# A fixed cycle for the pieces of each group of tokens, kept in strict order on each engine

## The chip, the cores and the metric

The program runs on one NeuronCore of one Trainium2 chip. The metric is the device time of one execution in microseconds (us), as the median of several runs. Engines are named as in the profile: PE (TensorE matmul), PEld (TensorE weight load), DVE (VectorE), ACT (ScalarE), POOL (GpSimd), SP (the queue that issues DMAs).

## The reference

Attention over pooled keys, then a feed-forward layer, both for every token:

```python
kv_pool = kv.reshape(B, H // r, r, W // r, r, C).mean(axis=(2, 4))   # r = 4
k = v = kv_pool.reshape(B, -1, C) @ w_sr                             # 768 keys per batch
s = scale * (q @ k.transpose(0, 2, 1))
a = softmax(s)
x = a @ v
h = x @ w_in                                                         # 128 -> 2048
out = (h - tanh(h)) @ w_out                                          # 2048 -> 128
```

There are 4 batches of 12288 tokens, C = 128. The kernel uses that scores and hidden values are small: it computes the softmax as a linear part (a 128x128 matrix applied to q) and what exp leaves beyond it, and h - tanh(h) around a centre as a slope, a square and a cube.

## The kernel before, in words

Tokens go in 96 groups of 512 (24 per batch). One group has these pieces; a "piece" of 1024 columns is two matmuls into one tile `big` of two PSUM banks, and there are three `big` tiles in a ring for all pieces of all groups.

Attention (function `attention`; the line numbers are those before the change):
- `load_q` (SP, L698) brings q, `rounded_q` (POOL, L701) makes the rounded copy `qr`.
- three times: `scores` (PE, L717) fills a `big`; `exps` (ACT, L721) reads it into E; `beyond` (DVE, L724) reads E and `big` into r2 and frees the `big`.
- `shares` (PE, L741, six narrow matmuls), `copy_shares` (ACT, L746), `all_shares` (PE, L749), `share_left` (ACT, L761, writes t): the denominators.
- `straight` with Mn (PE, L752, a plain fp32 product) and three times `values` (PE, L757) accumulate into one bank; `apart` (DVE, L768) multiplies it by t into dl; `rounded` (POOL, L771) makes dr.

The three accumulators (den4, den, num) share one PSUM bank, the ring `x` with one buffer, in which the small products of a batch's preparation take their turns too.

Feed-forward (function `feed_forward`), eight units:
- `forth` (PE, L810) fills a `big`; for units 1 to 7 `square` (ACT, L814) and `cube` (DVE, L817) make r and free the `big`; for unit 0 ACT copies it (L821) and POOL does the rest in three operations (L824, L828 twice).
- `back` (PE, L850) accumulates every unit into the bank `acc`, to which a plain product with A adds (`straight`, L798); `result` (ACT, L859) takes it to o, and SP stores it.

Keys (`keys`) and the weights around a centre (`about_centre`) of the next batch are prepared among the groups of the batch before: keys are pooled from 12 loads on DVE (L373) and POOL (L367), then small products on PE (L424, L433, L450, L503, L563, L665), DVE scales weights (L619).

The order is set at build time. Every piece of work is entered in `Plan` with a step number (one group is 8 steps), an engine, a duration, what it reads and writes. `Plan.run` plays the plan forward: each engine takes, among its pieces that could start within `SOON` of the earliest, the one with the lowest step. The order that comes out is the order of the instructions in each engine's queue; on the chip each engine goes through its queue, and semaphores hold an instruction until what it needs is done. Tiles of a ring are given out in the order of their steps.

Of the kernel before, what the change touches and what calls it, by code (L numbers as in the profile page):

```python
# [47 lines left out]
class Plan:  # L48

    HOP = 0.1  # L50
    OWN = {"DVE": 0.16, "ACT": 0.02}
    SOON = 0.15

    def __init__(self, tc):
        self.tc = tc
        self.ops, self.tiles, self.rings = [], {}, {}
        self.names = {}

# [11 lines left out]
    def op(self, step, engine, us, emit, reads=(), writes=(), late=0.0, port=False, dma=0.0,  # L70
           name=None):
        i = len(self.ops)
        self.ops.append((step, engine, us, emit, late, port or engine == "POOL", dma))
        self.names[name] = i
        for keys, writes_it in ((reads, False), (writes, True)):
            for k in keys:
                k, part = k if isinstance(k, tuple) else (k, None)
                self.tiles[k]["by"].append((i, writes_it, part))

    def run(self, between):  # L80
# [6 lines left out]
        for t in self.tiles.values():  # L87
            for j, (i, w, part) in enumerate(t["by"]):
# [62 lines left out]
def attention_then_ffn(ctx: ExitStack, tc: tile.TileContext, q, kv, w_sr, w_in, w_out, out):  # L151
# [23 lines left out]
    def sb(key, tag, shape, dt=F32, step=0.0):  # L175
# [509 lines left out]

    def attention(g, s0):
# [17 lines left out]
        plan.op(s0 - 10, "SP", 0.5, load_q, (), (qs,), late=2.0, dma=0.65)  # L704
        plan.op(s0 - 3, "POOL", 0.63, rounded_q, (qs,), (qr,))
        for k in range(AN):
            s, e, r = (f"{x}.{g}.{k}" for x in ("s", "e", "r2"))
            at = s0 + k * ATT / AN
            big(s, at)
            sb(e, "E", [P, WIDE])  # L710
            plan.tile(r, "r2", BUFS["r2"], lambda: wk.tile([P, 2 * WIDE], F16, tag="r2", name="r2",
                                                           bufs=BUFS["r2"])[:, 0:WIDE])
# [14 lines left out]
            plan.op(at - 6, "PE", 0.465, scores, (kTr, qr), (s,), late=0.2)  # L727
            plan.op(at, "ACT", 1.03, exps, (s,), (e,), late=0.1)
            plan.op(at, "DVE", 1.22, beyond, (s, e), (r,), late=0.08)
        at = s0 + ATT  # L730
# [20 lines left out]
        def straight():  # L751
            PE.matmul(out=plan[num], lhsT=plan[Mn], rhs=plan[qs], start=True, stop=False)  # L752

        def values(k):
            for h in range(2):
                n = 2 * k + h
                PE.matmul(out=plan[num], lhsT=plan[vvr][:, n], rhs=half(plan[f"r2.{g}.{k}"], h),  # L757
                          start=False, stop=(n == KT - 1))
# [11 lines left out]
        def rounded():  # L770
# [3 lines left out]
        plan.op(at, "PE", 0.5, shares, ["ident"] + [f"r2.{g}.{k}" for k in range(AN)], (den4,),  # L774
                late=0.2)
        plan.op(at, "ACT", 0.6, copy_shares, (den4,), (d4,), late=0.1)
        plan.op(at, "PE", 0.235, all_shares, ("ident", d4), (den,), late=0.2)
        plan.op(at, "ACT", 0.69, share_left, (den,), (t,), late=0.1)
        plan.op(at + 1, "SP", 0.5, store_left, (t,), (f"left.{g}",), late=2.0, dma=0.02)
        plan.op(at + 0.5, "PE", 0.93, straight, (Mn, qs), (num,))  # L780
        for k in range(AN):
            plan.op(at + 0.5, "PE", 0.465, partial(values, k), (vvr, f"r2.{g}.{k}"), (num,), late=0.2)
        plan.op(at + 0.5, "DVE", 0.69, apart, (num, t), (dl,), late=0.08)
        plan.op(at + 1, "POOL", 0.63, rounded, (dl,), (dr,))
# [4 lines left out]
    def feed_forward(g, s0):  # L789
# [5 lines left out]
        sb(o, "o", [P, G])  # L795

        def straight():
            PE.matmul(out=plan[acc], lhsT=plan[Am], rhs=plan[dl], start=(g > 0), stop=(g == 0))  # L798

        if g:  # L800
            plan.op(s0, "PE", 0.93, straight, (Am, dl), (acc,))
        for n in range(UN):
            hp, u, r, v, z = (f"{x}.{g}.{n}" for x in ("h", "u", "r", "v", "z"))
            s = s0 + n - (2 if n in ON_POOL else 0)
            big(hp, s)
# [24 lines left out]
            plan.op(s - 6, "PE", 0.465, forth, (winr, dr), (hp,), late=0.2)  # L830
            back_at = s + 2
            if n in ON_POOL:
                sb(r, "rp", [P, WIDE], R32)
                sb(v, "v", [P, WIDE])
                sb(z, "z", [P, WIDE])
                plan.op(s, "ACT", 1.03, copy, (hp,), (v,), late=0.1)
                plan.op(s, "POOL", 1.05, moved_pool, (v,), (z,))
                plan.op(s, "POOL", 2.4, partial(times, z, z, v), (z, v), (z,))
                plan.op(s, "POOL", 2.4, partial(times, r, z, v), (z, v), (r,))
                back_at = s + 5  # L840
            else:
                sb(u, "u", [P, WIDE])
                plan.op(s, "ACT", 1.03, square, (hp,), (u,), late=0.1)
                sb(r, "r", [P, WIDE], R32)
                plan.op(s, "DVE", 1.22, cube, (hp, u), (r,), late=0.08)

            def back(n=n, r=r):
                for h in range(2):
                    f = 2 * n + h
                    PE.matmul(out=plan[acc], lhsT=plan[Wr][:, f], rhs=half(plan[r], h),  # L850
                              start=(g == 0 and f == 0), stop=(g > 0 and f == FT - 1))

            plan.op(back_at, "PE", 0.465, back, (Wr, r), (acc,), late=0.2)

        if g == 0:
            plan.op(s0 + UN + 1, "PE", 0.93, straight, (Am, dl), (acc,), late=0.2)
# [7 lines left out]
        plan.op(s0 + UN + 2, "ACT", 0.69, result, (acc, G0), (o,))  # L864
# [280 lines left out]
```

## Time and profile before

| | |
|---|---|
| median of 3 runs | 1433.41 us (1432.98 to 1434.4) |
| the profiled execution's own time | 1434.69 us |
| its span, first to last instruction | 1433.0 us |
| granted TensorE clock, mean | 0.996 |
| busy: PE, DVE, ACT, POOL | 96%, 88%, 85%, 55% |

Busy time is the share of the span in which an engine has an instruction in work. Matmuls overlap, so PE's share is not a measure of how fast it goes; what a piece costs PE is seen from the distance between starts. Idle time in front of an instruction is given in brackets with the instruction that ended it.

### The profile page before, as it was taken

The page shows a single profiled execution, that of the slowest core. Times are in us where ns is not written, and L with a number is a line of the kernel's source. Part 1 is how long each engine was busy: PE and PEld are TensorE (multiplying, and loading weights), DVE is VectorE, ACT ScalarE, POOL GpSimd, SP SyncE. Part 2 cuts the span into 40 slices and gives each one's busy share as a digit, 9 for nine tenths or more (in the row PEclk, how much of TensorE's full clock was granted, in tenths as well). Part 3 has the DMA queues.
Part 4 walks back from the last instruction along what each step waited for, and adds up shares of the span by engine and source line. Part 5 has one row for each costly group of instructions (what it writes and reads, how often), then busy time and mean ns, then how long its engine had stood idle before and what let it go on. Part 6 is the DMA issues. An engine that isn't in the chain of part 4 may idle for free.

```text
span 1433.0 us, 17640 instructions
## 1 busy us (share of the span) xinstructions
PE 1376.5 (96%) x5920; PEld 852.7 (60%) x5920; DVE 1255.7 (88%) x1250; ACT 1212.2 (85%) x1395; POOL 787.1 (55%) x692
## 2 busy tenths in 40 slices
PE   5899999999999999999899999999999999999997
PEld 4565555666555556666555556666655556555554
DVE  7978888899988887899888888889888888888886
ACT  4768898887889898888789988888889898898996
POOL 4765453576745544667654545485545445555453
PEclk9999999999999999999999999999999999999999
DMA  9231111023311110123211111021111111111100
GB/s 353 86 107 38 45 38 38 30 67 119 132 38 37 38 44 31 52 82 122 92 37 45 38 37 38 30 60 45 38 45 37 37 39 37 45 37 37 37 23 31
DMA packets 40370, 84.54 MB, mean 59 GB/s; under 512 B 5232, under 2 KB 7408, under 8 KB 40272
## 3 DMA queue, kind: packets, MB, share of 16 engines
q1 hardware_dynamic: 40272, 83.34, 17.6%
q8 instruction: 49, 0.80, 0.2%
q14 instruction: 49, 0.40, 0.1%
HBM read 57.93 MB, written 25.39 MB: 58 GB/s over the span
## 4 chain that ended last, share of the span: by engine, by line
PE 75%; DVE 13%; POOL 4%; DMA 3%; issue 2%; ACT 2%; SPq 0%; DVEq 0%; POOLq 0%; ACTq 0%
PE big L810 23%; PE acc L850 18%; PE x L757 8%; PE big L717 7%; DVE r L724 6%; PE acc L798 5%; PE x L752 5%; PE x L741 3%; DVE dl L768 3%; DVE r L817 3%; DMA kc<-in_kv_dram 2%; PE x L749 1%; POOL kc L367 1%; POOL rp L828 1%; POOL z L828 1%
## 5 line engine op out<-in xcount | busy, mean ns | idle before, releaser
L817 DVE SCALAR_TENSOR_TENSOR r<-big,u 128x1024 fp32r<-128x1024 f32 x672 | 797.6, 1218 | 66.5 <-ACT u L814 57.7
L814 ACT ACTIVATE u<-big 128x1024 f32<-128x1024 f32 x672 | 682.9, 1036 | 107.1 <-PE big L810 100.6
L810 PE MATMUL big<-dr,winr 128*128 128x512 f32 x1536 | 579.8, 460 | 27.7 <-DVE r L724 17.6
L850 PE MATMUL acc<-r,Wr 128*128 128x512 f32 x1344 | 445.4, 424 | 1.1 <-DVE r L817 1.1
L810 PEld LDWEIGHTS big<-dr,winr 128*128 128x128 f32 x1536 | 262.3, 188 | 238.5 <-DVE r L817 74.1
L824 POOL TENSOR_SCALAR z<-v 128x1024 f32<-128x1024 f32 x96 | 100.4, 1046 | 544.2 <-ACT v L821 544.2
L724 DVE SCALAR_TENSOR_TENSOR r<-E,big 128x1024 f16<-128x1024 f32 x288 | 348.9, 1212 | 22.2 <-ACT E L721 20.1
L721 ACT ACTIVATE E<-big 128x1024 f32<-128x1024 f32 x288 | 296.1, 1028 | 38.2 <-PE big L717 33.4
L850 PEld LDWEIGHTS acc<-r,Wr 128*128 128x128 f32 x1344 | 251.4, 189 | 70.8 <-DVE r L817 2.8
L828 POOL TENSOR_TENSOR z<-z,v 128x1024 f32<-128x1024 f32 x96 | 230.5, 2401 | 7.6
L828 POOL TENSOR_TENSOR rp<-z,v 128x1024 fp32r<-128x1024 f32 x96 | 230.2, 2398 | 0.9
L717 PE MATMUL big<-qr,kTr 128*128 128x512 f32 x576 | 195.6, 422 | 2.5 <-DVE r L817 1.6
L757 PE MATMUL x<-r,vvr 128*128 128x512 f16 x576 | 174.0, 384 | 0.0
L717 PEld LDWEIGHTS big<-qr,kTr 128*128 128x128 f32 x576 | 100.9, 188 | 59.6 <-DVE r L817 34.4
L821 ACT COPY v<-big 128x1024 f32<-128x1024 f32 x96 | 97.4, 1015 | 30.7 <-PE big L810 30.7
L768 DVE TENSOR_TENSOR dl<-x,t 128x512 f32<-128x512 f32 x96 | 66.2, 690 | 52.0 <-PE x L757 51.4
L798 PE MATMUL acc<-dl,A 128*128 128x512 f32 x192 | 99.4, 599 | 0.6 <-ACT o L859 0.6
L752 PE MATMUL x<-q,Mn 128*128 128x512 f32 x192 | 99.2, 598 | 0.7 <-ACT t L761 0.7
L757 PEld LDWEIGHTS <-vvr 128*128 128x128 f16 x576 | 34.3, 98 | 81.4 <-issue 80.7
L850 PE MATMUL acc<-rp,Wr 128*128 128x512 f32 x192 | 75.5, 474 | 0.0
L859 ACT ACTIVATE o<-acc,G 128x512 f32<-128x512 f32 x96 | 65.4, 681 | 4.0 <-PE acc L850 3.6
L701 POOL TENSOR_SCALAR qr<-q 128x512 fp32r<-128x512 f32 x96 | 61.4, 640 | 5.2 <-PE x L757 3.2
(169 smaller groups left out, 835.8 us busy)
## 6 DMA issues: line engine op xcount, KB each, us to landing
q<-in_q_dram SPq DMA_DIRECT2D x96, 256.0 KB
out_dram<-o SPq DMA_DIRECT2D x96, 256.0 KB
kc<-in_kv_dram SPq DMA_DIRECT2D x38, 512.0 KB
r<-in_kv_dram SPq DMA_DIRECT2D x8, 512.0 KB
kc<-inverse SPq DMA_DIRECT2D x12, 256.0 KB
u<-in_moe_w_in_dram SPq DMA_DIRECT2D x3, 512.0 KB
u<-in_moe_w_out_dram SPq DMA_DIRECT2D x3, 512.0 KB
left<-t SPq DMA_DIRECT2D x96, 2.0 KB
```

The costliest lines, as they stand in the source:

```text
L717: PE.matmul(out=half(plan[s], h), lhsT=plan[kTr][:, n * P : (n + 1) * P], rhs=plan[qr], start=True, stop=True)
L721: A.activation(out=plan[e], in_=plan[s], func=AF.Exp)
L724: V.scalar_tensor_tensor(out=plan[r], in0=plan[e], scalar=-1.0, in1=plan[s], op0=ALU.add, op1=ALU.subtract)
L752: PE.matmul(out=plan[num], lhsT=plan[Mn], rhs=plan[qs], start=True, stop=False)
L757: PE.matmul(out=plan[num], lhsT=plan[vvr][:, n], rhs=half(plan[f"r2.{g}.{k}"], h), start=False, stop=(n == KT - 1))
L768: V.tensor_tensor(out=plan[dl], in0=plan[num], in1=plan[t], op=ALU.mult)
L798: PE.matmul(out=plan[acc], lhsT=plan[Am], rhs=plan[dl], start=(g > 0), stop=(g == 0))
L810: PE.matmul(out=half(plan[hp], h), lhsT=plan[winr][:, f * P : (f + 1) * P], rhs=plan[dr], start=True, stop=True)
L814: A.activation(out=plan[u], in_=plan[hp], func=AF.Square)
L817: V.scalar_tensor_tensor(out=plan[r], in0=plan[hp], scalar=1.0, in1=plan[u], op0=ALU.add, op1=ALU.mult)
L828: PL.tensor_tensor(out=plan[to], in0=plan[x], in1=plan[y], op=ALU.mult)
L850: PE.matmul(out=plan[acc], lhsT=plan[Wr][:, f], rhs=half(plan[r], h), start=(g == 0 and f == 0), stop=(g > 0 and f == FT - 1))
```

## The change

No instruction is added or removed; the numbers that set the order are others, and so is the rule.

1. `Plan.op` takes `lane=True`. All pieces of `attention` and `feed_forward` on PE, ACT, DVE and POOL are entered so (not the DMAs). In `run`, the lane pieces of one engine are sorted by step, and each may start only after the one ahead of it in that sort. Work of `keys`, `about_centre` and the rest is not in a lane and is placed by step as before.
2. A table `AT` gives each piece a step relative to its group's own, attention from 21 steps ahead of it (q's rounding 37.5) to the result 10.43 after. Every group has the same, also the first three, which before were further ahead.
3. Tiles in SBUF that lane pieces use (E, r2, o, u, r, rp, v, z) are given out by these steps too; before they came in order of entry.
4. The terms of both accumulations are entered in order of their steps, so the first and last of them carry start and stop: the plain products no longer come first.
5. Durations and delays in the plan are others (`HOP` 0 for 0.1, `SOON` 0.05 for 0.15, 1.137 for a cube instead of 1.22, and so on); they act only on the order.

```diff
-    HOP = 0.1
+    HOP = 0
-    SOON = 0.15
+    SOON = 0.05
...
+        if lane:
+            self.lanes.setdefault(engine, []).append((step, i))
...
+        for lane in self.lanes.values():
+            lane.sort()
+            for (_, i), (_, j) in zip(lane, lane[1:]):
+                behind[j].add(i)
...
+    AT = dict(
+        forth=[-1.25, 0.84, 1.42, 2.30, 3.73, 4.46, 5.34, 7.38],
...
+        shares=-13.40, copy_shares=-12.64, all_shares=-11.68, left=-11.16, straight=-10.37,
...
-        plan.op(s0 - 10, "SP", 0.5, load_q, (), (qs,), late=2.0, dma=0.65)
-        plan.op(s0 - 3, "POOL", 0.63, rounded_q, (qs,), (qr,))
+        plan.op(s0 + AT["rounded_q"] - 7, "SP", 0.5, load_q, (), (qs,), late=2.0, dma=0.65)
+        plan.op(s0 + AT["rounded_q"], "POOL", 0.59, rounded_q, (qs,), (qr,), lane=True)
...
-        bank(den4, "x", at - 0.1)
+        bank(den4, "x", s0 + AT["shares"])
-        bank(den, "x", at)
-        bank(num, "x", at + 0.5)
+        bank(den, "x", s0 + AT["all_shares"])
+        bank(num, "x", s0 + min(AT["straight"], *AT["values"]))
...
-            attention(g, g * UN - ahead(g))
+            attention(g, g * UN)
```

In the changed kernel's lines scores are L735, beyond L742, shares L758, all_shares L766, straight L769 and L819, values L774, apart L785, forth L829, cube L836, back L867, and L672 is the product that was L665.

First place: VectorE over one calm group late in the program, from one `apart` to the next. Before:

```order
L768 TENSOR_TENSOR dl<-x,t 128x512
L724 SCALAR_TENSOR_TENSOR r_11456<-E,big 128x1024
L817 SCALAR_TENSOR_TENSOR r<-big,u 128x1024
L724 SCALAR_TENSOR_TENSOR r_11473<-E,big 128x1024
L817 SCALAR_TENSOR_TENSOR r<-big,u 128x1024 x3
L724 SCALAR_TENSOR_TENSOR r_11527<-E,big 128x1024
L817 SCALAR_TENSOR_TENSOR r<-big,u 128x1024 x3
L768 TENSOR_TENSOR dl<-x,t 128x512
```

and with the change:

```order
L785 TENSOR_TENSOR dl<-x,t 128x512
L836 SCALAR_TENSOR_TENSOR r<-big,u 128x1024
L742 SCALAR_TENSOR_TENSOR r_11471<-E,big 128x1024
L836 SCALAR_TENSOR_TENSOR r<-big,u 128x1024 x3
L742 SCALAR_TENSOR_TENSOR r_11525<-E,big 128x1024
L836 SCALAR_TENSOR_TENSOR r<-big,u 128x1024 x3
L742 SCALAR_TENSOR_TENSOR r_11568<-E,big 128x1024
L785 TENSOR_TENSOR dl<-x,t 128x512
```

The seven cubes and three `beyond` are the same; a cube now follows `apart`, where a `beyond` did, and the three `beyond` stand further apart.

Second place: TensorE in the calm, from a group's third scores to the next group's shares. Before:

```order
L717 MATMUL big<-qr,kTr 128x512 x2
L850 MATMUL acc<-r,Wr 128x512 x4
L810 MATMUL big<-dr,winr 128x512 x2
L850 MATMUL acc<-r,Wr 128x512 x2
L810 MATMUL big<-dr,winr 128x512 x2
L850 MATMUL acc<-r,Wr 128x512 x2
L810 MATMUL big<-dr,winr 128x512 x2
L741 LDWEIGHTS share
L741 MATMUL x<-r_7307,share 32x512
```

and with the change:

```order
L735 MATMUL big<-qr,kTr 128x512 x2
L867 MATMUL acc<-r,Wr 128x512 x2
L829 MATMUL big<-dr,winr 128x512 x2
L867 MATMUL acc<-r,Wr 128x512 x2
L829 MATMUL big<-dr,winr 128x512 x2
L867 MATMUL acc<-rp,Wr 128x512 x2
L867 MATMUL acc<-r,Wr 128x512 x2
L829 MATMUL big<-dr,winr 128x512 x2
L758 LDWEIGHTS share
L758 MATMUL x<-r_7305,share 32x512
```

Before, four `back` and three `forth` stand between the scores and the shares, two of the `back` right after the scores; now it is four `back` and three `forth`, with two `back` together later, one of them that of unit 0 (from rp), which before came after the shares.

Third place: TensorE at a batch change, around a product of the next batch's slopes (x<-Wg,winT). Before:

```order
L850 MATMUL acc<-r,Wr 128x512 x2
L810 MATMUL big<-dr,winr 128x512 x2
L717 MATMUL big<-qr,kTr 128x512 x2
L665 MATMUL x<-Wg,winT 128x128 x4
L810 MATMUL big<-dr,winr 128x512 x2
L850 MATMUL acc<-r,Wr 128x512 x4
L810 MATMUL big<-dr,winr 128x512 x2
L563 MATMUL x<-hb,wout_69 128x1 x4
L810 MATMUL big<-dr,winr 128x512 x2
```

and with the change:

```order
L867 MATMUL acc<-r,Wr 128x512 x2
L766 LDWEIGHTS share
L766 MATMUL x<-d_3035,share 128x512
L829 MATMUL big<-dr,winr 128x512 x2
L867 MATMUL acc<-r,Wr 128x512 x2
L672 MATMUL x<-Wg,winT 128x128 x4
L867 MATMUL acc<-r,Wr 128x512 x2
L829 MATMUL big<-dr,winr 128x512 x2
L769 MATMUL x<-q,Mn 128x512
L735 MATMUL big<-qr,kTr 128x512 x2
```

Before, the product stood among scores and `forth`, outside the span in which the group's own denominators and values hold the ring `x`; now it stands between all_shares (L766) and the plain product (L769), both of which use that ring.

More of the change, by code (lines that the diff above doesn't have):

```diff
@@ L828, in times @@
                 PL.tensor_tensor(out=plan[to], in0=plan[x], in1=plan[y], op=ALU.mult)
-            plan.op(s - 6, "PE", 0.465, forth, (winr, dr), (hp,), late=0.2)
-            back_at = s + 2
+            plan.op(s0 + AT["forth"][n], "PE", 0.465, forth, (winr, dr), (hp,), late=0.196, lane=True)
+            first, then = s0 + AT["first"][n], s0 + AT["then"][n]
             if n in ON_POOL:
[L833 to L840, printed above, removed]
-            else:
[L842 to L845, printed above, removed]
@@ L847, in back @@
-            def back(n=n, r=r):
-                for h in range(2):
[L849 to L856, printed above, removed]
+                sb(r, "rp", [P, WIDE], R32, step=then)
@@ L1070, in attention_then_ffn @@
     VL = 1.0
-    def ahead(g):
-        if g < 3:
-            return LEAD + (38, 33, EXTRA2)[g]
-        return LEAD - max(0, g - (NGT - 12)) * RAMP
     for b in range(B):
```

95 lines of the change are left out of this document (61 added, 34 removed).

## The prediction, made before the changed kernel was run

> **What bounds the kernel now.** I read four views: the page (busy shares, the chain that ended last), the times of one line that runs once per group (L859, the result), the timeline of one calm group, and the table of waits over ten such groups.
>
> ```profile
> span 1433.0 us, 17640 instructions
> ...
> PE 1376.5 (96%) x5920; PEld 852.7 (60%) x5920; DVE 1255.7 (88%) x1250; ACT 1212.2 (85%) x1395; POOL 787.1 (55%) x692
> ...
> PE 75%; DVE 13%; POOL 4%; DMA 3%; issue 2%; ACT 2%; SPq 0%; DVEq 0%; POOLq 0%; ACTq 0%
> ```
>
> TensorE looks full, but its busy time counts matmuls from start to modelled end, and these overlap. So the question is what a group of 512 tokens costs, and what its matmuls need. The results give the first: each row has a count and the first and last start.
>
> ```profile
> L859 ACT ACTIVATE o<-acc,G x2: 687/689/691, 81.3 to 101.9; 128x512 f32<-128x512 f32 x2
> ...
> L859 ACT ACTIVATE o<-acc,G x10: 679/682/691, 101.9 to 224.6; 128x512 f32<-128x512 f32 x10
> ...
> L859 ACT ACTIVATE o<-acc,G x14: 678/680/692, 224.6 to 419.6; 128x512 f32<-128x512 f32 x14
> ...
> L859 ACT ACTIVATE o<-acc,G x14: 679/681/687, 542.6 to 739.4; 128x512 f32<-128x512 f32 x14
> ...
> L859 ACT ACTIVATE o<-acc,G x20: 677/680/682, 1134.6 to 1394.9; 128x512 f32<-128x512 f32 x20
> ...
> L859 ACT ACTIVATE o<-acc,G x4: 680/682/687, 1394.9 to 1426.8; 128x512 f32<-128x512 f32 x4
> ```
>
> A calm group takes 122.7/9 = 13.63 and 260.3/19 = 13.70 us, say 13.65. While the next batch is prepared, a group takes 195.0/13 = 15.0 and 196.8/13 = 15.1 us. The first interval is 20.6 us, the last three are 31.9 us together.
>
> What the matmuls need is read from starts that follow without a wait:
>
> ```profile
> 78.01 0.61 PE L741 MATMUL x<-r,share 128*32 128x512 f16 x6
> 78.55 1.66 PE L850 MATMUL acc<-r,Wr 128*128 128x512 f32 x6
> ...
> 80.27 1.02 PE L798 MATMUL acc<-dl,A 128*128 128x512 f32 x2
> 81.13 1.12 PE L752 MATMUL x<-q,Mn 128*128 128x512 f32 x2
> ...
> 1261.64 0.63 PE L850 MATMUL acc<-r,Wr 128*128 128x512 f32 x2
> ...
> 1262.11 0.62 PE L810 MATMUL big<-dr,winr 128*128 128x512 f32 x2
> ...
> 1262.56 0.59 PE L752 MATMUL x<-q,Mn 128*128 128x512 f32 x1
> ```
>
> Two pairs take 0.92 us, so a pair 0.46; the two plain fp32 products 0.86 each; the six narrow share matmuls 0.54; the single all_shares half a pair, 0.23. A group has 22 pairs (3 scores, 3 values, 8 forth, 8 back): 22 x 0.46 + 2 x 0.86 + 0.54 + 0.23 = 12.6 us; 12.7 with the pair at 0.465, which I use. So about 0.95 us of each calm group is TensorE waiting. (The Trainium skill, page "TensorE: Matmul & The Clock Gate", section "Back-to-back issue gap", gives N/2.4 + 2.5 ns for a warm matmul, 0.43 us for a pair; the sum would be 22 x 0.035 = 0.8 us lower, 11.9. The rows show 0.46 at a granted clock of 0.996, and the measurement decides.)
>
> The waits are at one place, over ten calm groups (1200 to 1336.4 us):
>
> ```profile
> PEld big L810 <- DVE r L817: 7.3, 29, 0.3
> PEld big L810 <- DVE r L724: 6.8, 19, 0.4
> ...
> PEld big L717 <- DVE r L817: 4.2, 10, 0.4
> ```
>
> 58 times in ten groups the weight load ahead of a refill of a `big` tile waits for the VectorE operation that reads the old contents. There are three such tiles and eleven pieces per group, so half the refills are late. That VectorE operation in turn is late because VectorE stood idle earlier. The rows of one such group give the price of every hop:
>
> ```profile
> 1249.39 3.49 DVE L817 SCALAR_TENSOR_TENSOR r<-big,u 128x1024 fp32r<-128x1024 f32 x3
> ...
> 1252.55 0.62 PE L717 MATMUL big<-qr,kTr 128*128 128x512 f32 x2
> ...
> 1253.01 0.60 PE L757 MATMUL x<-r,vvr 128*128 128x512 f16 x2
> ...
> 1253.20 1.03 ACT L721 ACTIVATE E<-big 128x1024 f32<-128x1024 f32 x1 [0.29 <-PE big L717]
> ...
> 1253.72 0.69 DVE L768 TENSOR_TENSOR dl<-x,t 128x512 f32<-128x512 f32 x1 [0.84 <-PE x L757]
> ...
> 1256.59 1.21 DVE L724 SCALAR_TENSOR_TENSOR r<-E,big 128x1024 f16<-128x1024 f32 x1
> ...
> 1257.86 0.73 PE L810 MATMUL big<-dr,winr 128*128 128x512 f32 x2
> ...
> 1259.65 1.03 ACT L814 ACTIVATE u<-big 128x1024 f32<-128x1024 f32 x1
> ...
> 1260.71 1.22 DVE L817 SCALAR_TENSOR_TENSOR r<-big,u 128x1024 fp32r<-128x1024 f32 x1 [0.64 <-ACT u L814]
> ...
> 67.20 1.95 ACT L814 ACTIVATE u<-big 128x1024 f32<-128x1024 f32 x2 [0.33 <-PE big L810]
> ```
>
> TensorE start to ScalarE start: 0.65. ScalarE start to VectorE start: 1.06. VectorE start to the refill's start: 1.27. VectorE spacing back to back: (3.49 - 1.22)/2 = 1.13; ScalarE spacing: 1.95 - 1.03 = 0.92. A refill that waited lasts 0.73 instead of 0.62, since its weights were not loaded ahead: 0.11 us of TensorE each. VectorE is idle 0.84 before `apart` and 0.64 before a cube here; its own work is 10 x 1.13 + 0.69 = 12.0 us, ScalarE's at most 1212.2/96 = 12.6. TensorE is thus the largest sum, but the ring of three tiles sets the period.
>
> **The change, part by part.** No instruction is added or removed. Everything is order, so each term is a time between results.
>
> Calm groups. In the new cycle the tightest refill is that of the next group's first scores, which takes the bank of unit 1. The path: third scores, exps, beyond, cube of unit 1, refill: 0.65 + 1.06 + 1.13 + 1.27 = 4.11 us. In the same stretch TensorE has 8 pairs and the shares: 8 x 0.46 + 0.54 = 4.22. The refill of unit 7's bank is the other: from the third scores through six full and three half ScalarE operations (6 x 0.92 + 3 x 0.5, the half ones an estimate from the full one), then 0.65 + 1.06 + 1.13 + 1.27, 11.1 us in all, against 19 pairs, two plain products, shares and all_shares, 11.2. So both come due about 0.1 us ahead, where the old order has six late refills per group. `apart` comes right after the last values, 0.7 us from their start as now (1253.01 to 1253.72); VectorE has 0.7 us to spare per group (12.7 - 12.0). I take TensorE's 12.7 plus one weight load uncovered, 0.1: 12.8 us. Bounds: 12.7 (nothing late) and 13.65 (nothing gained); it is nearest the lower, because the two chains fit by the rows. What hides VectorE's 12.0 us and ScalarE's is now TensorE's work itself; if one of them slips, there is nothing behind it to fill the gap, since each lane is strict. Late next would be `apart`, and behind it the cube of unit 7.
>
> Batch changes. Three times the next batch's keys and weights are prepared among the groups. Their prices:
>
> ```profile
> 30.49 3.73 PE L503 MATMUL acc<-col,win 128*128 128x1 f32 x32 [0.25 <-DVE col L420]
> 34.08 1.80 PE L424 MATMUL big<-kvp,wsr 128*128 128x384 f32 x4
> 35.68 2.76 PE L433 MATMUL big<-wsr,kvp 128*128 128x128 f32 x12
> 38.09 1.43 PE L717 MATMUL big<-qr,kTr 128*128 128x512 f32 x4
> ...
> 603.45 0.95 PE L563 MATMUL x<-hb,wout 128*128 128x1 f32 x8
> 604.26 0.71 PE L810 MATMUL big<-dr,winr 128*128 128x512 f32 x2
> ...
> L619 DVE TENSOR_TENSOR winr<-win,kc 128x512 fp32r<-128x512 f32 x4 | 4.9, 1234 | 0.0
> ...
> L373 DVE TENSOR_REDUCE kvp<-kc 128x64 f32<-128x1024 f32 x6 | 7.3, 1210 | 1.6 <-DMA kc<-in_kv_dram 1.6
> ```
>
> TensorE: L503 3.6, L424 1.6, L433 2.4, and 76 small ones (L563, L665, L450) at 0.81/8 = 0.1: 15.3 us per batch. VectorE: 7.3 + 4.9 and about 2 of small ones, 14. With TensorE full, its 15.3 all lie on the path. VectorE has 0.7 us to spare per group, 9 over the 13 groups, so about 5 of its 14 come on top. Of the fifteen small products that borrow the one-bank ring `x`, about seven now fall between a group's shares, all_shares and values, where the old order had hardly any room between; each must be drained by VectorE, at up to 1.13 us of waiting, before the next matmul in line, partly under the pair that stands between (0.46): some 0.6 us each, 4 to 5 us. Sum 25 us per batch over the calm period. Bounds: 15.3 (all else hidden) and 15.3 + 14 + 7 x 1.13 = 37. I stay in the middle, since VectorE's slack is real but the insertions are lumps.
>
> POOL, SP: the q loads and roundings are issued some 14 steps earlier, but a tile of q is reused only when the plain product of four groups before has read it; POOL is 55% busy and its result is now wanted 6 steps (some 10 us) after `rounded`. Cost nothing; if a load comes late, the two multiplies behind it on POOL move, and `back` of unit 0 has 8 us of room.
>
> Start. Second result 101.9 us now, with 7 us in the first interval beyond a calm group. Attention of groups 0 and 1 is no longer pulled ahead of the weights, and no forth may pass the second scores of group 2. I take 98; bounds 95 (all 7 gone) and 104 (two more VectorE operations ahead of the first result).
>
> End. The last three intervals stay 31.9, which is 6.5 less than three of 12.8; the closing test costs 0.9 (260.3 against 19 x 13.65), and 6.2 us follow the last result (1433.0 - 1426.8).
>
> Sum: 98 + 94 x 12.8 (1203.2) + 3 x 25 (75) + 0.9 - 6.5 + 6.2 = 1376.8 us of span. This execution took 1434.69 us beside its span of 1433.0, and the median of the runs is 1433.41, 0.4 above the span: 1377 us.
>
> **Rivals.** All late refills vanish, and VectorE's extra work finds room: period 12.7, 16 per batch, start 95: 95 + 1193.8 + 48 + 0.6 = 1337. For it: both chains fit. Against: both fit by 0.1 us only.
>
> Batch changes at the upper bound, 37 each: 1377 + 36 = 1413. For it: two L672 products stand directly ahead of the plain product that needs their bank. Against: the old order paid only 15.0 - 13.65 = 1.4 us per group there, little over TensorE's share.
>
> The period is set by the hops, not the order, and stays 13.65 with the old losses: about 1433, no change. Against: VectorE's idle 0.84 and 0.64 in the row come from values and squares ordered late.
>
> Slower: in a strict cycle without slack every refill comes a little late, so each of the eleven pays its weight load: 12.7 + 11 x 0.11 = 13.9, which gives 98 + 1306.6 + 75 + 0.6 = 1480. It decides from a period of 13.4, that is seven of eleven late. For it: six are late today; 0.1 us of room in two chains is as large as the weight load. Against: nine others have more room, and lateness of VectorE shrinks as soon as TensorE slows. Half of it, five late, gives 13.25 and 1419. (The same page of the Trainium skill, section "Architectural detail", says that TensorE only pulls weight loads ahead and keeps matmuls in order, and that the other engines are strict queues; the 0.73 against 0.62 agrees. By that rule a late piece delays all behind it, which speaks for this rival.)
>
> **The numbers.** Forecast (1352 to 1402) 0.52; floor 0.16; dear batch changes 0.11; five late 0.09; unchanged 0.04; slower 0.08. A difference under 0.2% (2.9 us) can't be told from none. The range 1340 to 1418 leaves out the slower, the unchanged, the five late and the lowest tail. Faster 0.88, same 0.04, slower 0.08.
>
> **What would show it.** L859 at a spacing near 12.8 in calm stretches, near 14.7 in batch changes; waits of the weight loads for VectorE far under 18 us in ten groups; L819 and L829 with few idle notes; VectorE idle under 1 us per group. Wrong if calm spacing stays over 13.3, or if after each L672 the plain product waits 2 us or more.

## The result and the profile after

| | before | changed |
|---|---|---|
| median | 1433.91 us (4 runs, 1432.98 to 1434.84) | 1393.53 us (4 runs, 1391.8 to 1394.07) |
| ratio | | 0.9716, 95% interval 0.97 to 0.9733 |
| profiled execution: time, span | 1434.69, 1433.0 | 1394.07, 1392.3 |
| mean granted TensorE clock | 0.996 | 0.983 |

The change takes 40 us off, 2.8%. The forecast was 1377, 16.5 lower, with 1340 to 1418 around it. The same rows of the page as before, now of the changed kernel:

```profile
span 1392.3 us, 17512 instructions
...
PE 1345.4 (97%) x5920; PEld 871.9 (63%) x5920; DVE 1276.1 (92%) x1250; ACT 1203.2 (86%) x1395; POOL 784.6 (56%) x692
...
PEclk8779999999999999999999999999999999999999
...
PE 85%; DVE 6%; DMA 3%; ACT 2%; POOL 2%; issue 1%; SPq 0%; ACTq 0%; POOLq 0%; DVEq 0%
```

TensorE's share hardly moves, VectorE's rises from 88% to 92%, and in the chain VectorE falls from 13% to 6%. What has no counterpart before is the clock row: in the first three slices of 35 us the granted clock is well below full, where before it read 9 throughout:

```profile
PEclk9999999999999999999999999999999999999999
```

The result's starts (L878, one per group; count, then first and last start) give the time by stage:

```profile
L878 ACT ACTIVATE o<-acc,G x2: 680/682/685, 106.9 to 123.3; 128x512 f32<-128x512 f32 x2
...
L878 ACT ACTIVATE o<-acc,G x9: 674/685/688, 123.3 to 226.2; 128x512 f32<-128x512 f32 x9
...
L878 ACT ACTIVATE o<-acc,G x16: 681/688/689, 226.2 to 440.6; 128x512 f32<-128x512 f32 x16
...
L878 ACT ACTIVATE o<-acc,G x7: 682/682/688, 440.6 to 517.6; 128x512 f32<-128x512 f32 x7
...
L878 ACT ACTIVATE o<-acc,G x12: 687/688/688, 1200.5 to 1341.5; 128x512 f32<-128x512 f32 x12
```

The second result, at 101.9 before, now comes at 123.3: 21.4 us are lost at the start. A calm group takes 77.0/6 = 12.83 and 141.0/11 = 12.82 us. The fifteen groups of the first batch change take 214.4, that is 21.7 over fifteen calm ones taken at 12.845 (the median interval); the other two changes cost 21.1 and 18.2 in the same way. Measured between the same results before, the three changes became 8.0, 12.9 and 9.2 us shorter and the calm stretches and the end 32.0 together; less the 21.4 at the start that is the 40.7 between the spans.

The waits of the weight loads for VectorE in 14 calm groups (1109 to 1288 us):

```profile
PEld big L829 <- DVE r L836: 5.9, 27, 0.2
PEld big L735 <- DVE r L836: 5.5, 13, 0.4
```

40 late refills in 14 groups, 11.4 us; before it was 58 in ten groups, 18.3 us. Per group 2.9 instead of 5.8, and 0.8 us instead of 1.8.

Where the start goes shows in the timeline of TensorE (start, length, engine and line, count, and in brackets the idle time and what ended it):

```profile
49.88 0.39 PE L758 MATMUL x<-r,share 128*32 128x512 f16 x2 [1.73 <-DVE r L742]
...
53.27 0.61 PE L758 MATMUL x<-r,share 128*32 128x512 f16 x2 [1.87 <-DVE r L742]
...
56.63 2.07 PE L769 MATMUL x<-q,Mn 128*128 128x512 f32 x2 [1.15 <-ACT t L778]
...
71.28 1.25 PE L829 MATMUL big<-dr,winr 128*128 128x512 f32 x2
...
78.71 1.16 PE L672 MATMUL x<-Wg,winT 128*128 128x128 f32 x8 [0.57 <-DVE A L678]
81.16 1.05 PE L570 MATMUL x<-hb,wout 128*128 128x1 f32 x8 [1.30 <-DVE A L678]
82.47 2.07 PE L672 MATMUL x<-Wg,winT 128*128 128x128 f32 x8 [0.25 <-DVE G L577]
84.93 1.87 PE L570 MATMUL x<-hb,wout 128*128 128x1 f32 x8 [0.38 <-DVE A L678]
87.04 1.87 PE L570 MATMUL x<-hb,wout 128*128 128x1 f32 x8 [0.25 <-DVE G L575]
89.16 1.87 PE L570 MATMUL x<-hb,wout 128*128 128x1 f32 x8 [0.25 <-DVE G L575]
91.28 1.04 PE L758 MATMUL x<-r,share 128*32 128x512 f16 x6 [0.25 <-DVE G L575]
```

Two things. Up to 71 us the attention of the first groups goes through the engines one step at a time, with TensorE waiting for each; the first `forth` starts at 71.28 (before at 55.97). Then six of the first batch's eight small products stand in a row (78.71 to 91.28), each waiting until the one ahead has left the single bank of ring `x`. The next group's shares use that ring too and come behind them, and in the strict order nothing of the cycle may pass the shares. ScalarE shows it as one hole:

```profile
92.36 0.59 ACT L763 CAST d<-x 128x512 f16<-128x512 f32 x1 [14.31 <-PE x L758]
```

Before the change the first `forth` came early, and the same eight products stood apart, with `forth`, scores and `back` between them:

```profile
55.97 0.70 PE L810 MATMUL big<-dr,winr 128*128 128x512 f32 x2 [1.09 <-DVE r L724]
...
71.01 0.71 PE L810 MATMUL big<-dr,winr 128*128 128x512 f32 x2
71.55 1.15 PE L665 MATMUL x<-Wg,winT 128*128 128x128 f32 x8
72.46 0.71 PE L717 MATMUL big<-qr,kTr 128*128 128x512 f32 x2
73.01 0.62 PE L810 MATMUL big<-dr,winr 128*128 128x512 f32 x2
73.47 0.95 PE L563 MATMUL x<-hb,wout 128*128 128x1 f32 x8
```

The eight matmuls that take 0.95 here (L563) take 1.87 in the last three of that row (L570); the granted clock there is treated in the last section.

### The profile page after: what moved, and what is told of

Its sections match the earlier page's. It is cut to its first block, busy times and chain, and to the rows that moved or that the text cites. A ratio compares the mean times of both kernels' runs of the same rounds, so it can differ in the third digit from the quotient of the medians.

```text
span 1392.3 us, 17512 instructions
## 1 busy us (share of the span) xinstructions
PE 1345.4 (97%) x5920; PEld 871.9 (63%) x5920; DVE 1276.1 (92%) x1250; ACT 1203.2 (86%) x1395; POOL 784.6 (56%) x692
## 4 chain that ended last, share of the span: by engine, by line
PE 85%; DVE 6%; DMA 3%; ACT 2%; POOL 2%; issue 1%; SPq 0%; ACTq 0%; POOLq 0%; DVEq 0%
PE big L829 24%; PE acc L867 23%; PE big L735 10%; PE x L774 9%; PE x L769 6%; PE acc L819 6%; PE x L758 3%; DVE r L836 2%; DVE r L742 2%; PE x L766 2%; DMA kc<-in_kv_dram 1%; ACT E L739 1%; PE x L570 1%; ACT u L833 1%; DVE kvp L380 1%
## 5 line engine op out<-in xcount | busy, mean ns | idle before, releaser
L836 DVE SCALAR_TENSOR_TENSOR r<-big,u 128x1024 fp32r<-128x1024 f32 x672 | 798.2, 1218 | 32.6 <-ACT u L833 26.9
L829 PE MATMUL big<-dr,winr 128*128 128x512 f32 x1536 | 568.5, 451 | 4.6 <-DVE r L742 2.7
L867 PE MATMUL acc<-r,Wr 128*128 128x512 f32 x1344 | 423.8, 408 | 1.1 <-DVE r L836 1.1
L843 POOL TENSOR_SCALAR z<-v 128x1024 f32<-128x1024 f32 x96 | 101.0, 1052 | 513.8 <-ACT v L840 513.8
L742 DVE SCALAR_TENSOR_TENSOR r<-E,big 128x1024 f16<-128x1024 f32 x288 | 351.1, 1219 | 39.6 <-ACT E L739 17.9
L829 PEld LDWEIGHTS big<-dr,winr 128*128 128x128 f32 x1536 | 276.8, 190 | 129.9 <-DVE r L836 38.0
L867 PEld LDWEIGHTS acc<-r,Wr 128*128 128x128 f32 x1344 | 251.7, 188 | 65.3 <-DVE r L836 2.4
L735 PE MATMUL big<-qr,kTr 128*128 128x512 f32 x576 | 232.1, 484 | 1.0 <-ACT winr L658 0.7
L774 PE MATMUL x<-r,vvr 128*128 128x512 f16 x576 | 175.9, 388 | 0.0
L735 PEld LDWEIGHTS big<-qr,kTr 128*128 128x128 f32 x576 | 101.9, 190 | 97.7 <-issue 44.0
L769 PE MATMUL x<-q,Mn 128*128 128x512 f32 x192 | 100.4, 604 | 2.4 <-ACT t L778 2.3
L819 PE MATMUL acc<-dl,A 128*128 128x512 f32 x192 | 99.5, 600 | 0.6 <-ACT o L878 0.6
L774 PEld LDWEIGHTS <-vvr 128*128 128x128 f16 x576 | 33.9, 99 | 79.4 <-issue 79.2
L785 DVE TENSOR_TENSOR dl<-x,t 128x512 f32<-128x512 f32 x96 | 66.3, 691 | 9.8 <-PE x L774 4.9
L763 ACT CAST d<-x 128x512 f16<-128x512 f32 x96 | 56.4, 587 | 19.0 <-PE x L758 19.0
L878 ACT ACTIVATE o<-acc,G 128x512 f32<-128x512 f32 x96 | 65.9, 686 | 5.9 <-PE acc L867 5.7
L758 PE MATMUL x<-r,share 128*32 128x512 f16 x576 | 59.8, 389 | 7.4 <-DVE r L742 6.0
```

What stands on the lines that cost most here:

```text
L735: PE.matmul(out=half(plan[s], h), lhsT=plan[kTr][:, n * P : (n + 1) * P], rhs=plan[qr], start=True, stop=True)
L742: V.scalar_tensor_tensor(out=plan[r], in0=plan[e], scalar=-1.0, in1=plan[s], op0=ALU.add, op1=ALU.subtract)
L758: PE.matmul(out=plan[den4][at : at + QUAD], lhsT=share[:, 0:QUAD], rhs=half(plan[f"r2.{g}.{k}"], h), start=(n < 4), stop=(n + 4 >= KT), ti ...
L829: PE.matmul(out=half(plan[hp], h), lhsT=plan[winr][:, f * P : (f + 1) * P], rhs=plan[dr], start=True, stop=True)
L836: V.scalar_tensor_tensor(out=plan[r], in0=plan[hp], scalar=1.0, in1=plan[u], op0=ALU.add, op1=ALU.mult)
L867: PE.matmul(out=plan[acc], lhsT=plan[Wr][:, 2 * n + h], rhs=half(plan[r], h), start=(start and h == 0), stop=(stop and h == 1))
```

## The experiments

Twelve kernels, each a variation of the changed one. Each ratio is to the kernel before, run on the same chip beside it (1433.9, 1433.3 and 1434.3 us in the three sets of runs); the changed kernel has 0.9716.

### The start

**Attention of groups 0 and 1 entered earlier** (e1_early):

```diff
-            attention(g, g * UN)
+            attention(g, g * UN - (36, 31, 0)[g] if g < 3 else g * UN)
```

> The changed kernel, with attention of groups 0 and 1 entered 36 and 31 steps earlier (as far ahead as the order before the change had them); all else, the strict lanes too, as in the change. Theory A (the start lost its 21 us in two parts: attention of the first groups begins after the weights' products and then runs piece after piece in a strict lane with TensorE idle and its clock down, and eight small products stand in one row in the bank ring x): the first part goes, so the first result comes near 97 us instead of 106.9 and the time is near 1384. Rival B (the first groups are limited by the sum of work ahead of the first result, however ordered): the first result stays within 2 us of 106.9, time 1393. Rival C (what is gained at the start is given back because the later groups then wait): first result near 97, time 1393.

1389.71 us, 0.9692 (0.9676 to 0.9708); first result at 101.8, second at 118.5. Of the 9.5 us that theory A expected, 3.8 came, so none of the three theories fits. In this run's timeline attention begins earlier, but the first `forth` still starts at 71.38, and the next group's shares still come behind the row of products, at 86.95.

**The eight small products spread** (e2_spread): two of the slopes' products go ahead of the first group's units and two among them, the four of L570 behind them.

```diff
-        slopes_at = [known + 7 + AS * n if b else n / 2 - SL for n in range(4)]
-        value_at = [known + 5 + AS * n if b else n / 2 + VL for n in range(4)]
+        slopes_at = [known + 7 + AS * n if b else (-6.5, -6.3, 0.6, 0.8)[n] for n in range(4)]
+        value_at = [known + 5 + AS * n if b else 8.6 + n / 8 for n in range(4)]
```

> The changed kernel, with the first batch's eight small products in the ring x (L672 four times, L570 four times) given other steps: two of L672 between the values of group 0 and the shares of group 1, two after group 1's values, the four L570 after group 2's values; all else as in the change. Theory A: the stretch from 78.7 to 91.3 us of the profile, in which TensorE does little but these products one by one, shrinks from 12.6 to about 4 us, and the first result comes near 97 us, time near 1385. Rival D (these products are slow only because TensorE's clock is halved there, and the halved clock comes from the thin work before): the products keep about 2 us each wherever they stand, time 1390 or more.

1382.28 us, 0.9639 (0.9623 to 0.9655). The result's row, and one of the products with a `forth` right behind it:

```profile
L878 ACT ACTIVATE o<-acc,G x2: 681/684/687, 94.3 to 112.3; 128x512 f32<-128x512 f32 x2
...
87.44 0.95 PE L570 MATMUL x<-hb,wout 128*128 128x1 f32 x8
88.25 0.70 PE L829 MATMUL big<-dr,winr 128*128 128x512 f32 x2
```

11 of the 21 us lost at the start come back, and nothing else moves (batch changes 22.2, 21.3, 18.6). So parting the row of products gives back half of the loss. The product lasts 0.95 again, so rival D, by which each keeps about 2 us wherever it stands, falls; the clock in the start rose along with it, though (last section).

**Both edits** (e3_both):

> Both edits of the start together: attention of groups 0 and 1 earlier, and the eight small products spread. Theory A: the two losses add, the first result comes near 86 us, time near 1374 (1393.5 - 20), granted clock near 1 from 50 us on. Rival (the two are one loss seen twice): the time is that of the better of the two alone.

1384.84 us, 0.9657 (0.9641 to 0.9673), second result at 114.9: 2.6 us longer than the spread alone. The two causes don't add; with the products apart, earlier attention gains nothing.

**Groups 0 to 2 out of the strict order** (e9_lane3), in all entries of `attention` and `feed_forward`:

```diff
-            plan.op(s0 + AT["scores"][k], "PE", 0.465, scores, (kTr, qr), (s,), late=0.196, lane=True)
+            plan.op(s0 + AT["scores"][k], "PE", 0.465, scores, (kTr, qr), (s,), late=0.196, lane=g >= 3)
```

> Groups 0 to 2 are freed from the strict cycle (each engine may take their pieces by step number as other work allows); from group 3 on nothing changes. Theory S (part of the 25 us at the start is the strict order itself: scores, shares and values of groups 0 and 1 go in turn through the three engines while TensorE waits up to 1.9 us per hop): the two groups overlap, the first result comes 5 to 12 us before 106.9, the second 5 to 10 us before 123.3, total 1382 to 1389. Rival W (the attention waits for the weights' products, and the eight small products in a row hold the rest, whatever the order of the cycle): first and second result within 2 us of the changed kernel's, total 1392 to 1396. Calm period 12.82 and the batch changes 21, 21, 18 in both.

1385.17 us, 0.9669 (0.9652 to 0.9685); first result at 97.3, second at 115.0, with the steps of the products left as they are. So strictness itself costs 8 us here, as theory S expected. Without it other pieces come between the products, ahead of the waiting shares:

```profile
81.77 1.71 PE L570 MATMUL x<-hb,wout 128*128 128x1 f32 x8
83.33 1.20 PE L867 MATMUL acc<-r,Wr 128*128 128x512 f32 x2
84.33 1.70 PE L570 MATMUL x<-hb,wout 128*128 128x1 f32 x8
```

**Spread, and groups 0 to 2 free** (e12_lane2):

> The eight small products spread, and groups 0 to 2 freed from the strict cycle. Theory A (two causes in the start, the hold by the products and the strict order): first result 86 to 90, total 1374 to 1379. Rival B (one stretch of TensorE's wait, which either edit fills): first result 92 to 96, total 1380 to 1386.

1381.96 us, 0.9644 (0.963 to 0.9657). The first result in its profiled execution is earlier still (90.9), the second 109.5, but over five runs the time is that of the spread alone. By the total, rival B holds: there is one stretch of waiting, and either edit fills much the same part of it. The first result lies between the ranges of the two theories.

### Strictness against the table of steps

**No strict order anywhere, the new steps kept** (e4_nolane):

```diff
         if lane:
-            self.lanes.setdefault(engine, []).append((step, i))
+            pass
```

> The whole strict cycle is taken away, the new step numbers stay. Theory C (the calm gain of 0.83 us a group comes from the fixed order): order by step numbers lets refills of big drift late again, the calm period goes back to 13.2 to 13.7, total 1425 to 1475, though the start is 5 to 10 us shorter. Rival N (the new step numbers alone give the calm gain, the strictness only fixes what they would give anyway): calm within 0.1 of 12.82, the start shorter by 5 to 10 us, total 1382 to 1390.

1390.59 us, 0.9688 (0.966 to 0.9716), four runs between 1384.15 and 1394.72. Neither theory was right as a whole: the start is 7 us shorter (second result 116.3), and the calm period doesn't go back to 13.2 but to 12.98 in two of its stretches, and stays at 12.82 in the rest:

```profile
L878 ACT ACTIVATE o<-acc,G x7: 680/681/682, 433.4 to 511.3; 128x512 f32<-128x512 f32 x7
```

77.9 for six groups against 77.0. So of the 0.83 us that a calm group gained about 0.7 come from the new step numbers (and the plan's new durations, which no run took apart from them) in those two stretches, and all of it in the others; strictness adds 0.16 in the two, 2.8 us over their 19 groups. In the profiled execution the program without strict order is 7.0 us shorter at the start and 7.8 longer after it: those 2.8, and the rest in the batch changes and at the end. That execution is the longest of the four; their median is 2.9 us below the changed kernel's, so over the whole program no gain of strictness is shown.

### What sets 12.8 us

**The plain product with Mn left out** (e5_nostraight): 0.86 us of TensorE's work less in every group; the linear part of the attention is missing from the output.

```diff
-        terms.append((AT["straight"], 0.857, straight, (Mn, qs)))
```

> The plain fp32 product with Mn is left out (so the linear part of the attention is missing from the output); nothing else changes. It costs TensorE 0.86 us a group and no other engine anything. Theory T (TensorE's own work sets the calm period, everything else just fits): the calm period falls by most of 0.86, to 12.0 to 12.3, until VectorE's 12.0 us of work per group takes over. Rival H (the hops through the three big tiles set it): 12.6 to 12.85, since the hops don't get shorter.

1380.31 us in one run. Twelve calm results (L877 there):

```profile
L877 ACT ACTIVATE o<-acc,G x12: 687/688/689, 1188.6 to 1329.3; 128x512 f32<-128x512 f32 x12
```

140.7/11 = 12.79 instead of 12.82. Theory T falls: 7% less work on TensorE shortens the calm group by 0.03. (Of the 13 us in the total about half are the start, where the second result comes at 116.4.) The chain of waits of this run over one group shows what holds it:

```profile
1246.57 0.70 PE big L828 x2
...
1251.57 0.95 PE acc L866 x4
...
1253.13 1.02 ACT u L832
...
1256.92 1.04 ACT u L832
...
1257.99 1.24 DVE r L835
...
1259.36 0.70 PE big L828 x2
```

A loop: a refill of `big` and 6 us of TensorE in its order up to the last `back`; the result and then squares and exps on ScalarE without a gap, to 1257.96; one cube; and the next group's refill, 12.79 us after the last. The product with Mn doesn't lie in this loop. In the changed kernel the chain from 1160 to 1183 us is TensorE from end to end:

```profile
1160.91 0.54 PE x L758 x6
1161.45 0.67 PE big L735 x2
...
1166.86 0.45 PE big L735 x2
```

Its pairs take 0.46 there, which makes the 12.6 of TensorE's own work; the one dearer pair is the next group's first scores, a late refill at 0.67, and with these 0.2 it is 12.8. From 1210 to 1338 us (busy times of PE, PEld, DVE, ACT, POOL, then the granted clock), first of the changed kernel, then without Mn:

```profile
1210.00:1338.00 128.00, 128.00 (x551) 81.68 (x550) 123.54 (x111) 121.10 (x141) 68.77 (x50) 1.00 0.11 38
...
1210.00:1338.00 128.00, 126.13 (x531) 76.16 (x530) 122.87 (x111) 121.85 (x142) 68.79 (x48) 1.00 0.09 30
```

TensorE has no idle time in the first, and 1.87 us in the second. So two limits stand 0.03 us apart: TensorE's work with that late refill, and this loop through three engines. That the loop holds 12.79 is shown; that TensorE would stay at 12.8 with a shorter loop is not, since no run shortened it.

### The batch changes

**Small products out of the gap between shares and values** (e6_ring): the preparation's steps are shifted so that none falls between a group's shares, all_shares and values.

```diff
-    FS, AS, WS, APART, MORE = 3, 8, 6, 3, 3.0
+    FS, AS, WS, APART, MORE = 4, 8, 6, 3, 3.0
-    KEYS, ABOUT, GAP = 105, 85, 8
-    KEYS1, ABOUT1, GAP1 = 80, 60, 6.5
+    KEYS, ABOUT, GAP = 106, 86, 8
+    KEYS1, ABOUT1, GAP1 = 82, 62, 6.5
```

> The changed kernel with the steps of the three later batch preparations moved by 1 or 2, and the four first products 4 steps apart instead of 3, so that each small product in the ring x falls after a group's values and ahead of the next group's shares, and none between shares, all_shares and values. Theory E (of the 21 us that a batch change costs, 15 to 16 are TensorE's own work and the other 5 are matmuls held in line behind a small product's bank): a batch change costs about 17, time near 1381. Rival F (the rest is VectorE's extra work, which stays): time within 2 us of 1393.5. Rival G (what a product costs is that it takes TensorE while the other engines run dry, wherever it stands): no change either, but VectorE waits right behind each product.

1406.26 us, 0.9798 (0.9782 to 0.9815): 13 us longer than the changed kernel, which none of the three theories expected; the changes cost 25.4, 27.2 and 22.3. The trace has no small product left in that gap, where the changed kernel has eight of the fifteen in each change. In the groups that lose most, VectorE's scaling of weights meets POOL's products:

```profile
957.66 4.46 DVE L626 TENSOR_TENSOR winr<-win,kc 128x512 fp32r<-128x512 f32 x2
...
959.40 1.86 POOL L668 TENSOR_TENSOR Wg<-wout,hb 128x512 f32<-128x512 f32 x1
```

**The same, with scaling and POOL's products at their old steps** (e7_ring2): on top of the last edit:

```diff
+        late = b and min(b, 2)
-        winr_at = known + 8 if b else s0
+        winr_at = known + 8 - late if b else s0
```

and `late` is taken from the steps of `third_at`, `first_order` and `by_first` likewise.

> As the run that moved the small products out of the gap between shares and values, but the steps of the scaling of winr, the slopes' third operand and the first-order part stay where the changed kernel has them, so that VectorE's scaling (two SBUF inputs) no longer meets POOL's products of two SBUF inputs. Theory K (that run's 12.7 us of loss is the meeting of these operations, 4.46 us for two scalings against some 2.0): batch changes 19 to 22, total 1388 to 1395. Theory R (the ring of x tiles: small products out of the gap save 3 us per change once the meeting is gone): 1382 to 1388. Rival Q (the moved steps themselves cost, by what else they displace): 1400 to 1407 again.

1401.97 us, 0.9785 (0.9768 to 0.9801); changes 24.8, 24.4, 19.9. That is in rival Q's range, but the steps alone did not part the two kinds of work, so theories K and R were not put to the test. The scaling starts 17 us after its load was issued, and what put it there no run shows:

```profile
308.17 1.07 SPq L620 DMA_DIRECT2D kc<-inverse  x2
...
325.38 4.47 DVE L627 TENSOR_TENSOR winr<-win,kc 128x512 fp32r<-128x512 f32 x2
```

So what the gap in ring `x` costs stays open in these runs: neither separates it from the meeting. What they do show is that a shift of the preparation by one or two steps costs 1.7 to 6.1 us a change.

**All pooling of batches 1 to 3 on POOL** (e8_pool):

```diff
-            if (j % 2 if b else j % 3 == 2):
+            if (b or j % 3 == 2):
```

> The pooling of the key and value blocks of batches 1 to 3, of which every second step goes to VectorE (L380, 3 to 4 us of VectorE in a batch change), goes to POOL altogether. Theory V (half of a batch change is VectorE work that displaces the fixed order by its own length: groups 18 and 19 lose 2.5 and 1.0 us where four L380 stand): the second and third batch change drop from 21 and 18 to 15 to 18 each, total 1386 to 1390. Rival P (batch changes are TensorE's own extra products, 15 us, and ring waits; VectorE's extra work fits into its 8% idle): batch excess unchanged, 1392 to 1396. Below that: POOL's longer pooling delays its fixed pieces (partials of 2.41 us): 1396 to 1405.

1387.43 us, 0.9683 (0.9667 to 0.9699). The total is in theory V's range, but not by its way: the changes cost 19.1, 19.5 and 18.2 instead of 21.7, 21.1, 18.2, and the largest part is the second result, which comes at 117.4, since batch 1 is pooled in the start. What left VectorE in the first change:

```profile
L380 DVE TENSOR_REDUCE kvp<-kc 128x64 f32<-128x1024 f32 x6 | 7.3, 1214 | 0.3 <-DMA kc<-in_kv_dram 0.2
```

7.3 us of work cost 2.7, and in the second change 1.6: most had hidden in VectorE's spare time. The third change, in which nothing is pooled, doesn't move.

### Together

**Spread and pooling on POOL** (e10_both):

> The two edits that each helped alone: the first batch's eight small products spread apart (11.3 us alone) and all pooling of batches 1 to 3 on POOL (6.1 us alone). Theory A (the first edit works in the start, the second in the batch changes and on VectorE in the start, and they add where they don't meet): 1376 to 1380. Rival B (both shorten the same wait in the start, and only the 4 us at the batch changes come on top): 1378 to 1384. Over 1384: they hinder each other, as the two edits of the start did.

1379.65 us, 0.9622 (0.9608 to 0.9635), which lies in the range of theory A and of rival B. The second result decides: it comes at 112.4, with the spread alone at 112.3, with the pooling alone at 117.4. So the start counts once, as rival B has it.

**And groups 0 to 2 free** (e11_all):

> The eight small products spread, all pooling of batches 1 to 3 on POOL, and groups 0 to 2 freed from the strict cycle. If the three causes are separate: first result 84 to 90, batch changes 19, 19.5, 18, total 1367 to 1375. If the start is one stretch that any of them fills: first result 90 to 96, total 1376 to 1382.

1376.64 us, 0.96 (0.9587 to 0.9613), the fastest of all: 2.8% faster became 4.0%. Second result at 109.2, changes 19.0, 19.9, 18.5. First result (90.2) and total lie at the lower end of what was expected from one stretch. Freeing the groups gives 3.0 us here, where it gave nothing on top of the spread alone, so it is not wholly the same stretch; what the difference is stays open. The start is still 7 us behind the kernel before.

## Why the prediction was right and wrong

**The start failed, and with it most of the miss.** The step was "Attention of groups 0 and 1 is no longer pulled ahead of the weights, and no forth may pass the second scores of group 2. I take 98". I booked the loss of the early attention as if only the first interval could shrink, with 104 as the upper end. It measured 123.3, 25.3 over. For the batch changes the prediction had put together that small products borrow ring `x` and that a strict order lets nothing pass; for the start it had not, though eight such products stand there and the four engines have little else in stock. The spread (11 us) and the freed groups (8 us) show both parts; they overlap. Pooling batch 1 on POOL takes 6 us off there too and doesn't add to the spread either; the prediction counted all pooling in the batch changes. What part of these is the clock is open.

**Calm groups: 12.8 against 12.82.** The mechanism, fewer late refills, is there (2.9 instead of 5.8 per group). I said TensorE's sum plus one weight load uncovered, 0.1, would set the period, with the two hop chains 0.1 us behind. TensorE's chain does run without a gap, but the run without Mn puts the second limit at 12.79: the room that I worked out as 0.1 is 0.03, and as a limit the loop is worth as much as TensorE. The price of a late refill, 0.11 from the lengths of two instructions, was too low: the late scores take 0.67 of the chain and not 0.46, 0.2 more. With pairs at 0.46 and not 0.465 the two sizes cancel in part, so that 12.8 is this near is partly luck. The rival "set by the hops, not the order" was wrong that nothing would be gained, and right that hops are a limit. Over 94 intervals the rest of the calm term is +3.8 us (12.84 as the median of all).

**Batch changes: 25 each against 21.7, 21.1, 18.2**, together 14.0 less. Some of TensorE's products can be priced from single groups of the profile after: the group with L424 and L431 is 1.57 us longer than a calm one, that with both dozens of L440 and L457 2.86, that with 24 of L510 2.92, where the prediction's prices give 1.6, 3.6 and 2.7. TensorE's 15.3 is thus about right. For VectorE's 5 on top and the 4 to 5 of ring `x` together, 6.4 and 5.8 us are left in the first two changes, of which 2.7 and 1.6 are the pooling, and 2.9 in the third. The two terms were too large together. In the third change, where nothing is pooled, 2.9 is left for the ring and for VectorE's scaling, less than the ring's 4 to 5, if TensorE's 15.3 holds. Two intervals between results there (964.8 to 979.8, and on to 993.9) hold, beyond the usual pieces, little but eight matmuls of L672 with eight of L570, and eight of L672. They are 2.13 and 1.24 longer than a calm one, where 0.1 a matmul gives 1.6 and 0.8: some 0.5 us beyond its own work for each product of L672, an estimate, near the prediction's 0.6. How the miss divides between the two terms, no run measured.

**POOL and SP: nothing, right.** POOL's idle time in the calm is all in front of its first piece, waiting for ScalarE's copy (POOL z L843), and no scores wait for a q load.

**End:** tail -6.7 against -6.5, closing test 1.5 against 0.9, 6.1 after the last result against 6.2.

Sum with the measured terms: 123.3 + 94 x 12.84 + 61.0 + 1.5 - 6.7 + 6.1 = 1392.2 (span 1392.3). Against the forecast: start +25.3, calm +3.8, changes -14.0, the rest +0.3. The sum came within 16 us because two errors of opposite sign met, which is luck: with the start's error and without that of the changes it would have been 1406, still inside the range but outside the forecast's own band of 1352 to 1402.

**Floor, dear changes, slower:** none came. Nor did the sign that was named for dear changes: after the start the plain product's waits come to 0.1 us in all. Five late refills of eleven at 0.11 each were feared; 2.9 came late, and what they cost is inside the 12.82.

## What to carry to other kernels

A fixed cycle is tuned for the steady state; look separately at the stretch where it fills, for there a strict order turns every single-buffered resource into a queue that nothing passes, and exempting the first rounds is cheap. When a period equals one engine's sum, don't conclude that this engine is the only limit: take a piece of its work away and see whether the period follows. In the steady state most of the gain came from numbers that put pieces in the right order; forcing the order was worth at most a fifth of it, in two of five calm stretches, and lost 7 to 8 us at the start.

## What the runs showed of the hardware

**TensorE's granted clock fell in the start, where TensorE waits.** Windows of 20 us from 60 to 100 (busy times of PE, PEld, DVE, ACT, POOL, then the granted clock), first of the changed kernel:

```profile
60.00:80.00 20.00, 15.64 (x61) 8.54 (x58) 12.81 (x15) 9.82 (x12) 10.22 (x11) 0.78 0.40 131
80.00:100.00 20.00, 17.45 (x68) 13.23 (x69) 7.54 (x14) 5.07 (x6) 8.52 (x13) 0.66 0.24 79
```

and of the kernel before:

```profile
60.00:80.00 20.00, 19.90 (x119) 14.97 (x117) 16.91 (x24) 14.10 (x16) 17.77 (x17) 1.00 0.30 94
80.00:100.00 20.00, 19.89 (x98) 12.98 (x98) 16.44 (x17) 12.21 (x15) 13.71 (x16) 1.00 0.46 145
```

The changed kernel's TensorE is 78% and 87% busy there, part of it matmuls that the slow clock itself stretches, and has a clock of 0.78 and 0.66; before, at 99%, it is 1.00. But the busy share alone doesn't settle the clock. The run with the products spread is 77% busy in the first of these windows and has 0.99:

```profile
60.00:80.00 20.00, 15.46 (x81) 9.60 (x80) 14.27 (x18) 11.39 (x14) 11.63 (x12) 0.99 0.40 131
```

So waits in the start can be paid twice, and part of the gains above may be clock (e11_all has 0.91, 0.91, 1.00, 1.00 in the windows from 20 to 100). How much of the 21 us that is, no run took apart. The Trainium skill, page "TensorE: Matmul & The Clock Gate", section "What's actually happening", says that the gate passes half the pulses after an idle window of about 3.4 us and all after a busy one, and that the window runs free of the program; a busy share is only an average over such windows. The rows agree that the clock falls where TensorE waits, but the longest wait of the changed kernel's TensorE from 40 us on is 1.87 us, well short of such a window; how little work makes a window idle, no run here shows. The four runs without strict order went from 1384.15 to 1394.72 us at mean clocks from 0.991 to 0.983, the longer the lower.

**Two engines reading two operands from SBUF each hold one another up.** In e6_ring two scalings on VectorE, about 1.0 us each alone, took 4.46 while POOL multiplied, and POOL's product 1.86 instead of 1.04. The Trainium skill, page "SBUF — State Buffer", section "SBUF: two separate sides", names a port pair that VectorE (with two SBUF inputs) and GpSimd lock by turns for a whole instruction; the times agree. Whether this is what the shifted preparation costs, the two runs don't separate.
